# Other step costs in a planner, a later ranking of the experts, and a last block in two halves

## The chip, the cores and the metric

The kernel runs on one core of a Trainium2 chip. Its time is the device time of one execution in microseconds (us), a median over runs. The core's engines run beside each other and wait for one another through semaphores: TensorE (PE in the profile; its weight loads are PEld), VectorE (DVE), ScalarE (ACT), GpSimd (POOL) and SyncE (SP), which issues most transfers. Each engine works through its own list of instructions strictly in order.

## The reference

Three parts follow each other. (1) Causal attention for 4 batches x 8 heads, 576 positions, head size 64, with a bias from a running sum. (2) A gated projection: five taps of a causal convolution give a gate, and the output is `(gate * (x @ w_val)) @ w_out`. (3) A layer of eight experts: each of 2304 tokens goes to one expert.

```python
bias = -(cum[:, :, :, None] - cum[:, :, None, :])
scores = np.where(causal, -1e9, scale * q @ k.T + np.minimum(bias, 0.0))
x = softmax(scores) @ v                            # attention, 32 heads
for k in range(5): gate_pre += conv_w[k] * xp[:, k:k + S, :]
x = sigmoid(gate_pre) * (x @ w_val) @ w_out        # gated projection
e = fresh_e if s == 0 or local_gate[b, s] < 0.5 else prev_e
out[b, s] = p[e] * (np.maximum(x[b, s] @ w1[e], 0.0) @ w2[e])
```

## The kernel before

Products that need full precision are made of three products of split operands (a high part and a rest, names with `h` and `l`).

**First part.** It covers attention, projection, logits and routing. The 32 heads are taken as 16 pairs, numbered 0 to 15, four to a batch. For each pair: q and k are loaded, transposed on TensorE, split by ACT and DVE into the single tile `qk` (lines 531 and 535), and copied into `T_p`; from pair 7 on all six copies of a pair are transfers of SP (`COPY`, L600). Nine score tiles `s_p_u` (L659 to L683) are read by DVE, which writes `tt` and the row minima (L666, L690), go through the exponential on ACT (L699), are scaled on POOL (L724), transposed on TensorE (`t`, L736), copied by ACT to `PT0` and `PT1` (L746 to L754) and multiplied by v (`pv_p`, L789). ACT copies the result to `x_p` (L799), of which there are two buffers. `x_p` is split by POOL (`xh`, `xl`, L803 and L807) and goes through the five taps on DVE (`g_p`, L814 once and L816 four times) and the gate's function on ACT (L821). A buffer of `x` is free again when the taps and the split of its pair have read it.

For each batch b, eight groups `val_b` of 12 matmuls (L866) are made, each followed by `y` and `yl` on DVE (L872, L890) and `yh` on ACT. Then come the groups `x2_b` of 12 matmuls (L927): the second half of the columns with the logits (`lgs`, L939), and the first half. These groups belong to no pair, so they can stand between the steps of later pairs. `route(b)` finds the expert and the slot of each token (L986 to L1055).

**What sets the order.** Every piece is a `Step` with an engine, a cost, what it comes after, the buffers that it holds (`SIZES`), and a rank (`RANKS`, a table of offsets that puts a step relative to its pair; the taps have pair + 31.589, pv has pair - 2.111). `Plan.order` counts time forward: it keeps a free time for each engine, takes the ready step that can start first, the one of lowest rank among those an engine could start at once, and adds its cost. It doubles the cost of a TensorE step when the window before was filled too little. The order found is then written out; on the chip only the order is left of the costs.

**Routing of the last batch.** `rank` and `back` give the slots. `excess` sorts the experts by their load (`turns`), sixteen short DVE steps L1170 to L1187 after a small product `nb` (L1160). `match` (L1065) and `own` (L1073) find expert 0's tokens, `join` (L1077, L1079) writes their list `id0`. Then POOL gathers the first tokens' rows (`xg`, L1306).

**Second part.** `ffn` takes the experts in turn: `up` (L1344), `down` (L1419, or L1385 turned), `leave` (L1361 on DVE, L1363 on ACT, then a scatter of the rows by POOL, L1365). At the end `over` loads the count of left-over blocks into every engine's register (L1192) and branches on it (L1193).

Of the kernel before, what the change touches and what calls it, by code (L numbers as in the profile page):

```python
# [22 lines left out]
P = 128  # L23
# [13 lines left out]
def fv(ap):  # L37
    return ap.bitcast(F32)
# [131 lines left out]
def build(tc, q, k, v, s, w_val, conv_w, w_out, w_gate, w_local, w1, w2, out, dbg=None):  # L170
    nc = tc.nc
    with ExitStack() as ctx:
# [35 lines left out]

# [300 lines left out]
        def qk_main(p, nm, loaded, sn):  # L509
# [26 lines left out]
            t = add("PE", 1.05 if p in LAY else 0.43, turn, loaded, ready["ident"], qk_read.get((p - 1, ih)), on=[sn, sm])  # L536
            a = add("ACT", 0.5, hi, t, qk_read.get((p - 1, ih)), on=[sm])
            z = add("DVE", 0.62, lo, a, qk_read.get((p - 1, il)), on=[sm])
            return a, z
# [34 lines left out]
        def assemble(p, k_, q_, r_):  # L574
# [15 lines left out]
            for h in range(2):  # L590
                r = slice(64 * h, 64 * h + 64)
                hd[h] = []
                for n, (a, i, src) in enumerate(((0, 0, slice(1, 3)), (64, 0, slice(0, None, 2)), (0, 1, slice(1, None, 2)))):
# [3 lines left out]
                    def copy(a=a, i=i, src=src, r=r, h=h, how=how):  # L597
# [7 lines left out]
                        else:  # L605
                            nc.gpsimd.tensor_scalar(o, fv(z), 1.0, 1.0, ALU.mult, ALU.mult)
                    hd[h].append(add(*{"S": ("SP", 0.91), "A": ("ACT", 1.12), "D": ("DVE", 0.74), "P": ("Pool", 1.25)}[how],
                                     copy, begun, deps, on=[sT], lat=FAR if how == "S" else 0.17))
# [9 lines left out]
        def attention(p):  # L618
# [20 lines left out]
            def unit(u):  # L639
# [31 lines left out]
                else:  # L671
                    m = None
                    for z in range(2):
# [12 lines left out]
                        def least(z=z, c=c):  # L686
                            if z == 0:
# [151 lines left out]
            g_done[p] = add("ACT", 0.57, gate, m, on=[sg]), sg  # L839

# [6 lines left out]
        def value(b, ranks, after=None, sm_tag="m"):  # L847
# [5 lines left out]
            for i in range(8):  # L853
# [39 lines left out]
                m = add("PE", c_pe(12 * 288), prod, al, [x[0] for x in xd], [w_done[j] for j in range(4)],  # L893
                        on=[sm] + [sl for x in xd for sl in x[1]])
# [5 lines left out]
                h = add("ACT", c_act(288) + 0.14 * more, hi, e, w_conv if more else None, on=on)  # L900
                l_ = add("DVE", c_dve(288) + 0.065 * more, lo, h, on=on)
                y_steps.setdefault((b, z), []).extend([h, l_])

        def x2_tile(b, t, ranks):
# [11 lines left out]
            for c0, c1, rank in ((256, WO, ranks[0]), (0, 256, ranks[1])):  # L916
# [24 lines left out]
                def store(c0=c0, tl=tl):  # L941
                    if both:
# [5 lines left out]
                    nc.sync.dma_start(out=x2d[r:r + m, c0:c0 + 256], in_=tl["x2"][0:m])  # L948
                a = add("PE", c_pe(12 * (c1 - c0)), prod, y_steps[b, 0], y_steps[b, 1] if t > 1 else None,
                        y_steps[0, 1] if both else None, [w_done[j] for j in range(4, 8)],  # L950
# [134 lines left out]
        def route(b):  # L1085
# [71 lines left out]
        def excess(part):  # L1157
# [121 lines left out]
        def ffn():  # L1279
# [13 lines left out]
            def blocks(e):  # L1293
                return [(n, min(P, BUD[e] - P * n)) for n in range((BUD[e] + P - 1) // P)]
# [78 lines left out]
            def down_wide(e, h):  # L1373
# [30 lines left out]
                late.extend(lambda n=n, m=m: back(n, m) for n, m in blocks(e))  # L1404

            def down(e, h):

                if turned(e):
                    return down_wide(e, h)
                for n, m in blocks(e):  # L1410
                    ps = bank()
                    c = slice(P * n, P * n + m)
# [14 lines left out]
                    leave(e, n, m, ps, DM // 2 if e == E - 1 and last else DM if n % 2 else 0)  # L1427

# [113 lines left out]
```

## Time and profile before

| | |
|---|---|
| median of 3 runs | 638.65 us (638.48 to 641.74) |
| the profiled execution | 637.11 us |
| its span, first to last instruction | 635.3 us |
| granted TensorE clock, mean | 0.956 |
| busy share of the span: PE, DVE, ACT, POOL | 92%, 65%, 55%, 39% |
| first part, up to the first product of `ffn` | 385.5 us |

A row of a view by stretches gives the busy time of each engine in that stretch, with its number of instructions in brackets, the granted clock (1.00 is full, 0.50 half) and the share that the transfer engines were busy. A busy TensorE is not one at its peak.

### The profile page before, as it was taken

The page shows a single profiled execution, that of the slowest core. Times are in us where ns is not written, and L with a number is a line of the kernel's source. Part 1 is how long each engine was busy: PE and PEld are TensorE (multiplying, and loading weights), DVE is VectorE, ACT ScalarE, POOL GpSimd, SP SyncE. Part 2 cuts the span into 40 slices and gives each one's busy share as a digit, 9 for nine tenths or more (in the row PEclk, how much of TensorE's full clock was granted, in tenths as well). Part 3 has the DMA queues.
Part 4 walks back from the last instruction along what each step waited for, and adds up shares of the span by engine and source line. Part 5 has one row for each costly group of instructions (what it writes and reads, how often), then busy time and mean ns, then how long its engine had stood idle before and what let it go on. Part 6 is the DMA issues. An engine that isn't in the chain of part 4 may idle for free.

```text
span 635.3 us, 12047 instructions
## 1 busy us (share of the span) xinstructions
PE 587.1 (92%) x4104; PEld 518.7 (82%) x4104; DVE 413.1 (65%) x1024; ACT 347.8 (55%) x867; POOL 248.3 (39%) x376
## 2 busy tenths in 40 slices
PE   6697988999999999988989978999999999999993
PEld 5475766778778887867979978899898999999792
DVE  5589897888866898974779434435363636465440
ACT  4487786877667777755635304424343536355440
POOL 7367786642634365546541242030403003132101
PEclk8899798999999999989989969999999999999997
DMA  8877467766588787736044624355464637375610
GB/s 160 160 181 181 107 141 151 147 157 135 139 198 200 164 187 168 165 94 150 18 156 131 105 46 135 111 182 164 161 195 145 205 100 247 117 235 173 233 46 26
DMA packets 94244, 93.94 MB, mean 148 GB/s; under 512 B 62040, under 2 KB 68312, under 8 KB 94120
## 3 DMA queue, kind: packets, MB, share of 16 engines
q1 hardware_dynamic: 90244, 83.15, 51.3%
q0 software_dynamic: 3936, 9.99, 5.0%
q8 instruction: 34, 0.56, 0.4%
q14 instruction: 30, 0.25, 0.2%
HBM read 57.90 MB, written 10.79 MB: 108 GB/s over the span
## 4 chain that ended last, share of the span: by engine, by line
PE 60%; DVE 19%; issue 8%; DMA 7%; POOL 3%; ACT 2%; SPq 1%; POOLq 0%; DVEq 0%; ACTq 0%
PE h L1344 15%; PE h L1419 8%; PE h L1385 7%; PE x L927 5%; PE val L866 5%; PE pv L789 4%; DMA T<-qk 4%; DVE g L816 3%; PE t L736 3%; DVE tt L666 3%; PE s L659 2%; PE s L661 2%; PE xT L1321 1%; POOL tt L724 1%; DVE qk L535 1%
## 5 line engine op out<-in xcount | busy, mean ns | idle before, releaser
L724 POOL TENSOR_SCALAR tt<-tt,st 128x512 f32<-128x512 f32 (+1 forms) x144 | 99.8, 708 | 98.1 <-ACT tt L699 45.9
L1276 DVE TENSOR_TENSOR wl<-raw,wh 128x1024 fp32r<-128x1024 f32 x64 | 78.2, 1223 | 32.3 <-ACT wh L1273 31.5
L699 ACT ACTIVATE tt<-tt,st 128x512 f32<-128x512 f32 (+3 forms) x144 | 83.4, 581 | 21.8 <-DVE st L666 12.1
L1344 PE MATMUL h<-xth,wh 128*128 128x384 f32 (+5 forms) x256 | 76.0, 311 | 1.4 <-ACT xth L1323 1.4
L1344 PE MATMUL h<-xth,wl 128*128 128x384 f32 (+5 forms) x256 | 75.1, 308 | 0.0
L1365 POOL DMA_INDIRECT out_dram<-out,id x22 | 28.0, 1273 | 114.0 <-ACT out L1363 93.7
L736 PE MATMUL t<-ident,tt 128*128 128x128 f32 x384 | 64.8, 285 | 6.3 <-POOL tt L724 2.9
L666 DVE CUSTOM_DVE_ANT_0 tt<-s,mask 128x512 f32<-128x512 f32 (+3 forms) x128 | 59.0, 484 | 14.9 <-PE s L661 12.9
L1273 ACT ACTIVATE wh<-raw 128x1024 fp32r<-128x1024 f32 x64 | 66.7, 1053 | 0.0
L1349 DVE SCALAR_TENSOR_TENSOR hl<-h,hh 128x384 fp32r<-128x384 f32 (+5 forms) x64 | 31.2, 487 | 45.5 <-ACT hh L1348 45.3
L1348 ACT ACTIVATE hh<-h 128x384 fp32r<-128x384 f32 (+5 forms) x64 | 28.1, 438 | 57.9 <-PE h L1344 54.1
L816 DVE SCALAR_TENSOR_TENSOR g<-x,cw,g 128x576 f32<-128x576 f32 x64 | 58.3, 914 | 0.5
L736 PEld LDWEIGHTS t<-ident,tt 128*128 128x128 f32 x384 | 47.2, 146 | 13.6 <-POOL tt L724 6.2
L1306 POOL DMA_INDIRECT xg<-x2d,id x22 | 22.6, 1029 | 83.4 <-PE h L1402 42.6
L659 PE MATMUL s<-T 128*128 128x256 f32 (+2 forms) x128 | 48.8, 388 | 6.9 <-DVE st L690 5.0
L789 PE MATMUL pv<-PT,nv 128*64 128x320 f32 (+3 forms) x384 | 50.0, 392 | 2.3 <-ACT x L799 2.0
L1344 PEld LDWEIGHTS h<-xth,wh 128*128 128x128 f32 x256 | 48.1, 188 | 1.9 <-ACT xth L1323 1.6
L1344 PEld LDWEIGHTS h<-xth,wl 128*128 128x128 f32 x256 | 48.1, 188 | 0.2
L1344 PE MATMUL h<-xtl,wh 128*128 128x384 f32 (+5 forms) x256 | 47.7, 308 | 0.0
L661 PE MATMUL s<-T 68*128 68x256 f32 (+2 forms) x128 | 42.9, 344 | 3.0 <-DMA T<-qk 2.9
L789 PEld LDWEIGHTS pv<-PT,nv 128*64 128x64 f32 x384 | 26.2, 138 | 22.3 <-issue 4.1
L927 PE MATMUL x<-wo_h,yl 128*128 128x266 f32 (+3 forms) x144 | 43.1, 299 | 0.0
(236 smaller groups left out, 1577.5 us busy)
## 6 DMA issues: line engine op xcount, KB each, us to landing
raw<-in_moe_w_dram SPq DMA_DIRECT2D x64, 512.0 KB
T<-qk SPq DMA_DIRECT2D x76, 320.0 KB
nv<-in_v_dram SPq DMA_DIRECT2D x32, 128.0 KB
x2d<-x SPq DMA_DIRECT2D x32, 128.0 KB
nk<-in_k_dram SPq DMA_DIRECT2D x26, 128.0 KB
nq<-in_q_dram SPq DMA_DIRECT2D x26, 128.0 KB
wsc<-in_moe_w_val_dram SPq DMA_DIRECT2D x4, 512.0 KB
wsc<-in_moe_w_out_dram SPq DMA_DIRECT2D x4, 512.0 KB
```

Source lines behind the costliest of these rows:

```text
L659: nc.tensor.matmul(ps[:, 0:N], lhsT=Q[:, 0, P * t:P * t + P], rhs=K[:, 0, 0:N], start=True, stop=False)
L661: nc.tensor.matmul(ps[:, 0:N], lhsT=Q[0:68, 1, P * t:P * t + P], rhs=K[0:68, 1, 0:N], start=False, stop=True)
L666: nc.vector.tensor_tensor_reduce(out=tl["tt"][:, 0:W], in0=tl["ps"][:, 0:W], in1=mask[:, 512 - W:512], scale=1.0, scalar=3.0e38, op0=ALU.a ...
L699: nc.scalar.activation(tt[:, 0:W], tt[:, 0:W], AF.Exp, bias=st[:, 0, i:i + 1], scale=-1.0, accum_out=st[:, 1, i:i + 1])
L724: nc.gpsimd.tensor_scalar(tl["tt"][:, 0:W], tl["tt"][:, 0:W], st_["st"][:, 2, i:i + 1], 1.0, ALU.mult, ALU.mult)
L736: nc.tensor.transpose(ps[:, j], tl["tt"][:, P * j:P * j + P], ident)
L789: nc.tensor.matmul(tl["ps"][64 * h:64 * h + 64, half, c:c + w], lhsT=vt[0:K, j, h] if j < 4 else vr[:, 2 * hp + h], rhs=(PT1 if half else ...
L816: nc.vector.scalar_tensor_tensor(tl["g"], x[:, t:t + S], cw[:, hp, t:t + 1], tl["g"], ALU.mult, ALU.add)
L927: nc.tensor.matmul(ps[0:m, 0:c1 - c0], lhsT=yy[:, kc] if both else yy[:, kc, P * t:P * t + m], rhs=wt_[:, kc, c0:c1], start=n == 0, stop=n ...
L1273: nc.scalar.activation(hi, raw, AF.Copy)
L1276: nc.vector.tensor_tensor(lo, raw, fv(hi), ALU.subtract)
L1344: nc.tensor.matmul(ps[:, 0:N], lhsT=w[:, P * f:P * f + P], rhs=xx[:, kc, 0:N], start=n == 0, stop=n == 11)
```

## The change

Three edits.

1. The planner's costs. `c_pe`, `c_act`, `c_dve` and `c_pool` give a step other fixed parts and slopes, and single steps get other numbers: a tap of DVE 0.88 for 0.73 (the first one 0.8 for 0.4), POOL's split 0.72 and 1.5 for 0.65 and 1.36, the copies into `T` more on every engine. `RANKS`, `SIZES` and what comes after what are the same, so the instructions of the first part are the same and their order on each engine differs.
2. `nb` and `excess` come after `join`.
3. The last block of the last expert is made in two halves of 256 columns, each with its own copy (DVE for the first, ACT for the second) and its own scatter, and the count for `over` is loaded before the second copy.

```diff
-        def c_pe(n):
-            return n / 2350
+        def c_pe(n, k=2):
+            return n / 2400 + 0.0125 * k
         def c_act(n):
-            return 0.05 + n / 1200
+            return 0.12 + n / 1200
         def c_dve(n):
-            return 0.065 + n / 960
+            return 0.11 + n / 960
         def c_pool(n):
-            return 0.23 + n / 1000
+            return 0.35 + n / 950
...
-            a = add("Pool", 0.65, hi, xo, on=[sx, sh])
-            z = add("Pool", 1.36, lo, a, on=[sx, sh, sl])
+            a = add("Pool", 0.72, hi, xo, on=[sx, sh])
+            z = add("Pool", 1.5, lo, a, on=[sx, sh, sl])
...
-                m = add("DVE", 0.73 if t else 0.4, lambda t=t: tap(t), xo, m, ready["cw"], on=[sx, sg])
+                m = add("DVE", 0.88 if t else 0.8, lambda t=t: tap(t), xo, m, ready["cw"], on=[sx, sg])
...
-            add("DVE", 0.4, lambda: one[b].join(), m, base, on=[sm])
+            joined = add("DVE", 0.4, lambda: one[b].join(), m, base, on=[sm])
...
-            a = add("PE", 0.1, lambda: excess(0), ranked, on=[sm])
+            a = add("PE", 0.1, lambda: excess(0), ranked, joined, on=[sm])
...
+            def down_end(e, h, n, m):
...
+                for z in range(2):
+                    nc.vector.tensor_scalar(it2[0:m, z:z + 1], it[0:m, n, 0:1], 2, z, ALU.mult, ALU.add)
+                for z in range(2):
+                    ps = bank()
...
+                            nc.tensor.matmul(ps[0:m, 0:256], lhsT=a[:, c], rhs=w[:, r], start=k == 0, stop=k == 23)
...
+                    if z:
+                        fa["most"] = blocks_left()
...
+                    if z:
+                        nc.scalar.activation(o[0:m, 0:256], ps[0:m, 0:256], AF.Copy, scale=p)
+                    else:
+                        nc.vector.tensor_scalar(o[0:m, 0:256], ps[0:m, 0:256], p, None, ALU.mult)
+                    nc.gpsimd.memset(spare, 0.0)
+                    i = nc.gpsimd.indirect_dma_start(
+                        out=out.rearrange("b s (z d) -> (b s z) d", z=2),
...
```

Where the order moves, first DVE in the middle of the first part, around the last tap of pair 9 (`g_9`; `tt_p_u` is a score read of pair p, `y` and `yl` belong to a `val` group, `lgs` to an `x2` group). Before:

```order
L816 SCALAR_TENSOR_TENSOR g_9_3053<-x_9_2892,cw_97,g_9_3053 128x576
L690 ISA tt_11_2_3119,st_11_0_3079<-s_11_2_1_3157,mask4_82,st_11_0_3079 128x288
L690 ISA st_11_0_3079 128x1
L535 SCALAR_TENSOR_TENSOR qk_103<-qT_12_3149,qk_103 128x512
L666 ISA tt_11_3_3183,st_11_1_3182<-s_11_3_3174,mask_81 128x512
```

And in the changed kernel:

```order
L666 ISA tt_14_5_3710,st_14_1_3659<-s_14_5_3684,mask_81 128x256
L666 ISA st_14_1_3659 128x1
L872 SCALAR_TENSOR_TENSOR y_1_3_1_3712<-g_7_2544,val_1_3_1_3662 128x288
L816 SCALAR_TENSOR_TENSOR g_9_3542<-x_9_2802,cw_97,g_9_3542 128x576
L711 TENSOR_SCALAR st_14_1_3659<-st_14_1_3659 128x3
...
L939 COPY lgs_1_157<-x2_1_0_256_3727 128x9
L814 TENSOR_SCALAR g_10_3769<-x_10_3022,cw_97 128x576
L816 SCALAR_TENSOR_TENSOR g_9_3542<-x_9_2802,cw_97,g_9_3542 128x576
L939 COPY lgs_0_155<-x2_1_4_256_3752 64x9
L939 COPY lgs_1_157<-x2_1_4_256_3752 64x9
L816 SCALAR_TENSOR_TENSOR g_9_3542<-x_9_2802,cw_97,g_9_3542 128x576
```

The last tap of pair 9 stood among the score reads of pair 11; now it stands behind six of the nine score reads of pair 14.

Second, ACT at the end of attention, around the copy of pair 15's first product (`x_15`). Before:

```order
L746 ACTIVATE PT0_104<-t_15_7_4506 128x256
L933 ACTIVATE x2_2_1_256_4545<-x2_2_1_256_4513 128x256
L821 ACTIVATE g_14_4497<-g_14_4497 128x576
L799 ACTIVATE x_15_4566<-pv_15_4533 128x320
L746 ACTIVATE PT0_104<-t_15_8_4551 128x128
```

And in the changed kernel:

```order
L821 ACTIVATE g_13_4415<-g_13_4415 128x576
L799 ACTIVATE x_15_4531<-pv_15_4503 128x320
L746 ACTIVATE PT0_104<-t_15_7_4525 128x256
L746 ACTIVATE PT0_104<-t_15_8_4529 128x128
L933 ACTIVATE x2_2_1_256_4555<-x2_2_1_256_4534 128x256
L799 ACTIVATE x_15_4531<-pv_15_4503 128x256
L821 ACTIVATE g_14_4522<-g_14_4522 128x576
```

The gate of pair 14 (`g_14`) stood ahead of both copies of `x_15` and now stands behind them.

Third, DVE after the last batch's slots are known (`mx_3`): `sh_3` is the first of the sixteen steps of `excess`, `eq` are the five of `match`. Before, and then in the changed kernel:

```order
L1044 TENSOR_REDUCE mx_3_5020<-so_3_5129 128x5
L1170 SCALAR_TENSOR_TENSOR sh_3_5021<-nb_5137,pref_85 1x8
L1171 MEMSET sh_3_5021 1x1
...
L1187 CAST nbo_108<-sh_3_5021 1x8
L1065 TENSOR_SCALAR eq_0_5171<-slot_no_4614,mx_3_5020 128x384
```

```order
L1044 TENSOR_REDUCE mx_3_5020<-so_3_5129 128x5
L1065 TENSOR_SCALAR eq_0_5151<-slot_no_4593,mx_3_5020 128x384
...
L1079 TENSOR_TENSOR id0_89<-id0_89,own_5185 128x3 x2
L1171 SCALAR_TENSOR_TENSOR sh_3_5021<-nb_5205,pref_85 1x8
...
L1188 CAST nbo_108<-sh_3_5021 1x8
L1328 TENSOR_TENSOR xtl_0_5321<-xT_0_0_5322,xth_0_5320 128x4x128
```

The sixteen steps of `excess` moved from in front of `match` to behind `join`. The first gather of `ffn` waits, in both kernels, for the last DVE instruction that stands ahead of `ffn`: that was L1079, and is now L1188.

Counted over whole stretches of the order, cut behind the last scores of a pair: between pairs 0 and 7, 7 and 8, 8 and 13, 13 and 15, and behind pair 15 up to the last routing product `so_3`, TensorE's list held 6, 5, 20, 9 and 28 groups of `val` and `x2` (8 + 12 `val` + `x2` in the third, 6 + 3 in the fourth); it now holds 5, 3, 14, 14 and 32 (6 + 8 and 4 + 10). The products `pv_12` moved from the third to the fourth. DVE's list, cut behind the last score reads of the same pairs, held 24, 7, 20, 1 and 12 of the taps of L816; it now holds 19, 4, 13, 16 and 12. The fourth stretch also gets 5 more `yl`, 6 more `lgs` and a second routing.

## Rows read from the trace of the kernel before

**Rows 1.** Busy time by stretches; cut at last score reads of pairs 0, 7, 8, 13, 15

```profile
core 0: us, PE busy (x) PEld busy (x) DVE busy (x) ACT busy (x) POOL busy (x), PEclk, DMA share, GB/s
34.50:155.40 120.90, 109.33 (x782) 87.76 (x780) 105.20 (x304) 93.25 (x278) 75.69 (x101) 0.93 0.64 146
155.40:177.90 22.50, 21.71 (x166) 18.82 (x164) 20.50 (x55) 15.26 (x47) 14.48 (x18) 1.00 0.70 163
177.90:269.20 91.30, 89.18 (x682) 75.04 (x683) 72.56 (x237) 66.51 (x207) 43.93 (x67) 1.00 0.77 179
269.20:311.85 42.65, 38.84 (x284) 32.87 (x283) 27.22 (x97) 24.91 (x78) 20.16 (x36) 0.96 0.43 102
311.85:366.30 54.45, 52.45 (x413) 49.65 (x411) 41.10 (x92) 23.08 (x59) 18.05 (x25) 0.97 0.43 117
385.50:625.40 239.90, 238.27 (x1480) 222.19 (x1480) 119.91 (x159) 105.73 (x163) 48.35 (x62) 1.00 0.50 161
```

**Rows 2.** Chain of waits: start us, length us, engine, tile, line, instructions

```profile
182.65 2.35 PE pv L789 x20
186.64 0.80 PE pv L789 x8
189.04 1.42 PE x L927 x12
197.98 1.60 PE val L866 x12
477.30 11.13 PE h L1419 x48
578.47 1.38 PE h L1344 x12
```

**Rows 3.** The taps' line: instructions, duration ns min/median/max

```profile
L816 DVE SCALAR_TENSOR_TENSOR g<-x,cw,g x64: 781/819/1883, 49.5 to 332.6; 128x576 f32<-128x576 f32 x64
```

**Rows 4.** Timeline of POOL and of DVE: start us, length us, instructions

```profile
318.43 3.21 POOL L807 TENSOR_TENSOR xl<-x,xh 128x576 fp32r<-128x576 f32 x2
...
320.38 2.74 DVE L816 SCALAR_TENSOR_TENSOR g<-x,cw,g 128x576 f32<-128x576 f32 x2
```

**Rows 5.** Busy time by stretches of 2 us, behind pair 15

```profile
324.00:326.00 2.00, 0.08 (x1) 0.08 (x2) 0.89 (x2) 1.14 (x4) 0.00 (x0) 1.00 0.18 66
326.00:328.00 2.00, 2.00 (x14) 1.77 (x15) 0.52 (x1) 0.69 (x3) 0.54 (x1) 0.79 0.35 86
328.00:330.00 2.00, 2.00 (x11) 2.00 (x11) 1.26 (x2) 0.26 (x1) 1.94 (x4) 0.50 0.92 320
```

**Rows 6.** Timeline of ACT behind pair 15; in brackets idle time and releaser

```profile
324.86 0.68 ACT L821 ACTIVATE g<-g 128x576 f32<-128x576 f32 x1 [1.25 <-DVE g L816]
325.45 0.42 ACT L799 ACTIVATE x<-pv 128x320 f32<-128x320 f32 x1
```

**Rows 7.** Timeline of the last routing

```profile
366.47 0.15 DVE L1170 SCALAR_TENSOR_TENSOR sh<-nb,pref 1x8 f32<-1x8 f32 x1
...
369.22 0.28 PE L927 MATMUL x<-wo_h,yh 128*64 128x256 f32 x1
...
369.61 1.72 DVE L1065 TENSOR_SCALAR eq<-slot_no,mx 128x384 fp32r<-128x384 f32 x5
...
372.29 3.33 PE L1073 MATMUL own<-tv,eq 128*128 128x4 f32 x15 [2.79 <-DVE tv L1134]
...
376.62 1.01 POOL L1306 DMA_INDIRECT xg<-x2d,id  x1 [1.18 <-issue]
```

**Rows 8.** Timeline of the end

```profile
624.92 0.40 PE L1419 MATMUL h<-wh,hh 128*128 128x512 f32 x1
625.36 0.48 DVE L1361 TENSOR_SCALAR out<-h,id 128x256 f32<-128x256 f32 x1 [10.35 <-PE h L1419]
625.92 0.47 ACT L1363 ACTIVATE out<-h,id 128x256 f32<-128x256 f32 x1 [5.48 <-DVE out L1361]
626.67 0.98 POOL L1365 DMA_INDIRECT out_dram<-out,id  x1 [4.90 <-ACTq L1193]
```

More of the change, by code (lines that the diff above doesn't have):

```diff
@@ L536, in qk_main @@
             t = add("PE", 1.05 if p in LAY else 0.43, turn, loaded, ready["ident"], qk_read.get((p - 1, ih)), on=[sn, sm])
-            a = add("ACT", 0.5, hi, t, qk_read.get((p - 1, ih)), on=[sm])
-            z = add("DVE", 0.62, lo, a, qk_read.get((p - 1, il)), on=[sm])
+            a = add("ACT", 0.56, hi, t, qk_read.get((p - 1, ih)), on=[sm])
+            z = add("DVE", 0.66, lo, a, qk_read.get((p - 1, il)), on=[sm])
             return a, z
@@ L606, in copy @@
                             nc.gpsimd.tensor_scalar(o, fv(z), 1.0, 1.0, ALU.mult, ALU.mult)
-                    hd[h].append(add(*{"S": ("SP", 0.91), "A": ("ACT", 1.12), "D": ("DVE", 0.74), "P": ("Pool", 1.25)}[how],
+                    hd[h].append(add(*{"S": ("SP", 0.91), "A": ("ACT", 1.2), "D": ("DVE", 1.05), "P": ("Pool", 1.6)}[how],
                                      copy, begun, deps, on=[sT], lat=FAR if how == "S" else 0.17))
@@ L693, in least @@
                                 accum_out=st[:, 0 if z else 3, i:i + 1])
-                        o = add("PE", c_pe(4 * 288), prod, Td[0], Td[1], on=[sT, sp], rows=0.77)
+                        o = add("PE", c_pe(4 * 288, 4), prod, Td[0], Td[1], on=[sT, sp], rows=0.77)
                         m = add("DVE", c_dve(288), least, o, m, ready["mask"], on=[sp, stt, ss])
@@ L712, in rec @@
                     nc.vector.reciprocal(st[:, 2, 0:n], st[:, 1, 0:n])
-                r = add("DVE", 0.3, rec, exps, on=[ss])
+                r = add("DVE", 0.4, rec, exps, on=[ss])
                 for i in range(n):
@@ L837, in attention @@
             for t in range(5):
-                m = add("DVE", 0.73 if t else 0.4, lambda t=t: tap(t), xo, m, ready["cw"], on=[sx, sg])
-            g_done[p] = add("ACT", 0.57, gate, m, on=[sg]), sg
+                m = add("DVE", 0.88 if t else 0.8, lambda t=t: tap(t), xo, m, ready["cw"], on=[sx, sg])
+            g_done[p] = add("ACT", 0.64, gate, m, on=[sg]), sg
         yb, y_steps, y_free, lgs, lg_steps = {}, {}, {}, {}, {}
@@ L892, in value @@
                 gd, sg = g_done[b * NP + oc]
-                m = add("PE", c_pe(12 * 288), prod, al, [x[0] for x in xd], [w_done[j] for j in range(4)],
+                m = add("PE", c_pe(12 * 288, 12), prod, al, [x[0] for x in xd], [w_done[j] for j in range(4)],
                         on=[sm] + [sl for x in xd for sl in x[1]])
@@ L900, in value @@
                 h = add("ACT", c_act(288) + 0.14 * more, hi, e, w_conv if more else None, on=on)
-                l_ = add("DVE", c_dve(288) + 0.065 * more, lo, h, on=on)
+                l_ = add("DVE", c_dve(288) + 0.1 + 0.065 * more, lo, h, on=on)
                 y_steps.setdefault((b, z), []).extend([h, l_])
@@ L948, in store @@
                     nc.sync.dma_start(out=x2d[r:r + m, c0:c0 + 256], in_=tl["x2"][0:m])
[L949 removed]
+                a = add("PE", c_pe(12 * (c1 - c0), 12), prod, y_steps[b, 0], y_steps[b, 1] if t > 1 else None,
                         y_steps[0, 1] if both else None, [w_done[j] for j in range(4, 8)],
@@ L1189, in excess, with blocks_left @@
                 nc.sync.dma_start(out=nbd.rearrange("(o e) w -> o e w", o=1), in_=nbo)
+        def blocks_left():
+            return nc.values_load(most_, min_val=0, max_val=(NT - BUD[-1]) // P)
         def over():
-            most = nc.values_load(most_, min_val=0, max_val=(NT - BUD[-1]) // P)
+            most = fa["most"]
             with tc.If(most > 0):
@@ L1404, in down_wide @@
                 late.extend(lambda n=n, m=m: back(n, m) for n, m in blocks(e))
+            def down_end(e, h, n, m):
+                it = idt[e]
+                p = fv(it)[0:m, n, 1:2]
+                c = slice(P * n, P * n + m)
+                it2 = fx.tile([P, 2], I32, tag="it2", name="halves", bufs=1)
+                for z in range(2):
+                    nc.vector.tensor_scalar(it2[0:m, z:z + 1], it[0:m, n, 0:1], 2, z, ALU.mult, ALU.add)
+                for z in range(2):
+                    ps = bank()
+                    k = 0
+                    for f in range(8):
+                        wh, wl = wt[e, 4 + f // 2]
+                        r = slice(DM * (f % 2) + 256 * z, DM * (f % 2) + 256 * z + 256)
+                        hh, hl = h[f]
+                        for a, w in ((hl, wh), (hh, wl), (hh, wh)):
+                            nc.tensor.matmul(ps[0:m, 0:256], lhsT=a[:, c], rhs=w[:, r], start=k == 0, stop=k == 23)
+                            k += 1
+                    if z:
+                        fa["most"] = blocks_left()
+                    o = fx.tile([P, DM], F32, tag="o", name=f"out_{e}_{n}_{z}", bufs=3)
+                    if z:
[5 more added lines that the diff above has]
+                        out=out.rearrange("b s (z d) -> (b s z) d", z=2),
+                        out_offset=bass.IndirectOffsetOnAxis(ap=it2[0:m, z:z + 1], axis=0), in_=o[0:m, 0:256],
+                        in_offset=None, bounds_check=2 * NT - 1, oob_is_err=False)
+                    tc.declare_no_dep(i.ins, group="rows", reason="rows differ")
+                    tc.add_to_no_dep_group("rows", i.ins)
             def down(e, h):
@@ L1410, in down @@
                 for n, m in blocks(e):
+                    if e == E - 1 and n == len(blocks(e)) - 1:
+                        down_end(e, h, n, m)
+                        return
                     ps = bank()
@@ L1426, in down @@
                             w_next()
-                    leave(e, n, m, ps, DM // 2 if e == E - 1 and last else DM if n % 2 else 0)
+                    leave(e, n, m, ps, DM if n % 2 else 0)
             order = [(e, i) for e in range(E) for i in range(8)][4:]
```

## The prediction

> **What bounds the kernel now.** I read the busy time by stretches first, cut where DVE has read the last score of a pair, then the chain of waits, then the timelines of three places. The stretches [rows 1] are: S1 (pairs 0 to 7, 120.90 us), S2 (to pair 8, 22.50), S3 (to pair 13, 91.30), S4 (to pair 15, 42.65), S5 (from there to the last routing product, 54.45), then the last routing up to 385.5 us, then the experts (239.90). In S1 DVE has the least slack that matters: 105.20 of 120.90 us, 87%. In S2 and S3 TensorE does: 21.71 of 22.50 and 89.18 of 91.30, with DVE at 72.56 and the transfers at 0.77. S4 is TensorE again, 38.84 of 42.65, with DVE at only 27.22. S5 is TensorE, 52.45 of 54.45. The experts keep TensorE at 238.27 of 239.90 us at full clock. So the planner's order decides S1 to S5, 331.8 us in which the binding engine changes, and the two small edits decide some us at the joint and at the end.
>
> The total work does not change. Every gain of the first edit is idle time of the binding engine that goes away, or work that moves from a stretch where its engine binds to one where it does not.
>
> **First edit, stretch by stretch.** The prices: a `val` group takes 1.60 us of TensorE, an `x2` group 1.42, a pair's two pv products 2.35 + 0.80 = 3.15 [rows 2]; a tap 0.82 us of DVE (median) [rows 3].
>
> S1: DVE loses five L816 taps (24 to 19), one L814, one `y` and three `yl`, in all 5 x 0.82 = 4.1 plus about 2. With 87% of the stretch busy I count most of it: -5 us; bounds -6 (DVE paces all of it) and 0 (the chain of a pair paces it).
>
> S2: three `x2` groups leave and one `val` comes, -3 x 1.42 + 1.60 = -2.7 us of an engine busy 96% of the time. I take -2.5; bounds -3 and 0.
>
> S3: two `val` and four `x2` groups leave, and pair 12's products with them: -3.2 - 5.7 - 3.15 = -12.0 us of TensorE, 77.1 left. What is late next is ACT, 66.51 now and about 62 then, and the transfers, 0.77 x 91.30 = 70 us that do not shrink. At the share that TensorE has now the stretch would end 12.3 us earlier; the transfers would then be busy 89% of the time, more than in any stretch of rows 1, so I take -11. Bounds -12.3 and 0 (the copies into `T` pace the pairs).
>
> S4 pays. It gets two `val` groups less, seven `x2` more and pair 12's products, -3.2 + 9.9 + 3.15 = +9.9 us for TensorE (48.7). DVE gets fifteen taps, two first taps, five `yl`, six `lgs` and one routing: 15 x 0.82 = 12.3, and about 11 for the rest by the same line prices, so 27.2 + 23 = 50 us. DVE becomes the engine that ends last. At the 0.91 that TensorE reaches there now, 50 us make 55: +12.4. The near bound is 50.2 us, DVE without a gap (+7.6). The far one is the lowest share that DVE has in a neighbouring stretch where it also works through taps, `y` and routing, S5 with 41.10 / 54.45 = 0.755: 66 us (+23). I take 55 because S4, like S1, would have the score reads in between, and S1 runs at 0.87.
>
> Here a tap's price is weighed once more. Two taps under POOL's two splits took 2.74 us, 1.37 each, against the 0.82 of the median [rows 3, 4]. The Trainium skill (SBUF — State Buffer, section "SBUF: two separate sides") says why that would be: a DVE instruction with two inputs in SBUF and a GpSimd instruction take the same port pair in turns, and the loser blocks. The trace agrees with it here. By it the planner's fixed 0.88 for a tap is too low wherever POOL works; POOL would be busy some 32 us of S4's 55 (its 20.16 and about 12 for a second set of sends and three more splits), so 0.58 x 15 x 0.55 = 4.8 us more for S4 and 639.2 us in all. The sum below stays with 0.91, since S1's 24 taps under a POOL busy 75.69 of 120.90 us are part of its 87%.
>
> S5: four `val` groups more, +6.4 us. Against them, the stall behind pair 15: TensorE stands 1.92 us in 324 to 326, and the granted clock is 0.79 and 0.50 in the 4 us behind it, 2 x (0.21 + 0.50) = 1.4 us lost [rows 5]. It stands because ACT's copy of `x_15` at 325.45 is queued behind the gate of pair 14 at 324.86, which waited 1.25 us for the taps [rows 6]; in the new order that gate stands behind the copies. The four groups fill what is left of the stall, so 6.4 - 3.3 = +3.1; bounds 0 and +6.4.
>
> Sum of the first edit: -5 - 2.5 - 11 + 12.4 + 3.1 = -3.0 us.
>
> **Second edit.** `excess` takes 369.61 - 366.47 = 3.14 us of DVE ahead of `match` [rows 7]. Without it `match` starts 3.1 us earlier, its 1.72 us and the five short steps behind it end near 369.2, and `own` starts at 369.5, where TensorE's last `x2` matmul ends, instead of 372.29. That is 2.8 us earlier. But the gather now waits for the last instruction of `excess`, so the 3.14 us stand behind `join` again: own's end, 3.14, and the 1.0 us that lie between own's end and the gather now. With own's 3.33 us that gives 377.0, 0.4 later than 376.62. `own` ran there at half clock, after TensorE had stood for 2.79 us; where it follows the `x2` matmuls at once it may take half of its time, 1.7 us, and the gather starts at 375.3, 1.3 earlier. I take -0.8; bounds -1.3 and +0.4. `turns`, written some 5 us later, is first read for expert 1's weights, which are loaded behind the first products of `ffn`: hidden.
>
> **Third edit.** 48 matmuls of 256 columns for 24 of 512: 48 x 1.38 / 12 = 5.5 us against 24 x 11.13 / 48 = 5.6 [rows 2], so nothing. DVE's half and its scatter lie beside the second half's matmuls. After the last matmul ACT no longer waits for DVE's copy: now 625.36 to 625.92 passes before it starts [rows 8], then not. Gain 0.56; the count's loads are short and beside other work. The rest, from POOL's scatter to the end of the span, moves with it. I take -0.5; bounds -0.8 and 0. The two steps for the halved row numbers lie on DVE, which has stood 10.35 us there.
>
> **The total.** -3.0 - 0.8 - 0.5 = -4.3. Made against the profiled execution's own 637.11 us that is 632.8. The median of the runs shown is 638.65, 1.54 above it, and so the forecast is 638.65 - 4.3 = 634.4 us.
>
> **Rivals.**
>
> *Nothing moves.* The time that the binding engines need, DVE in S1 and S4 and TensorE elsewhere, is about the same in both orders (the sum of the moved amounts, with S4 at DVE's 50 us, is -6 - 2.7 - 12 + 50 - 38.8 + 6.4 = -3), and the gaps of S4 eat it. For it: S1 to S5 already run at 87 to 98% of the binding engine. Against it: the stall in S5 has a cause that the new order takes away. Time: 637.5.
>
> *Slower: the taps hold the pairs.* Place: S4, the last tap of pair 9. There are two `x` buffers, so pair 11's copy waits for it, pair 12's products for that copy, and so on to pair 15. DVE's list now has six score reads of pair 14, four `y` and their `yl` ahead of that tap, and behind it two routings, each a chain from TensorE over ACT to DVE during which DVE stands. If DVE gets under a share of about 0.80 of S4 (62 us) the first edit loses; at S5's 0.755 S4 takes 66 us, 11 more than I count. Time: 634.4 + 11 = 645.4. For it: a rank that puts the taps last, now with more of DVE's time known as taken. Against it: TensorE's groups lie there as filler, and S1 kept 0.87 with the same taps.
>
> *Much faster.* S1 to S3 reach their near bounds and S4 takes 52 us: -6 - 3 - 12.3 + 9.4 + 0 = -12, and -1.8 for the two other edits: 624.8. For it: dense attention leaves no engine over 90% in S3. Against it: transfers near 0.9.
>
> That the new costs leave the order nearly as it was is ruled out by the order itself.
>
> **How the numbers follow.** The forecast case, 630.5 to 637, has 0.42; nothing moves 0.19; slower 0.25; much faster 0.14. A measurement of this kernel tells about 0.5%, 3.2 us, from no change: below 635.5 is faster, above 641.8 slower. Faster: 0.14, four fifths of 0.42 and a little of the second, 0.50. Slower: 0.26 with the rival's own. Same: 0.24. The range, 623 to 646, reaches from the much faster case to the slower one; the far ends of all bounds together lie outside it.
>
> **What would show it.** In the changed profile: S3 (score reads of pair 8 to those of pair 13) near 80 us with the transfers above 0.80; S4 near 55 us with DVE above 0.85 busy; no standing of TensorE behind pair 15 and no half clock there; the first gather less than 9.6 us after the last routing product; ACT's last copy starting within 0.1 us of the last matmul. I am wrong if S3 does not shrink by more than 5 us, or if S4 takes more than 62.

## The result, and the profile after

The changed kernel takes 644.56 us (median of 16 runs, 640.05 to 649.26) against 640.25 us for the kernel before (16 runs). The ratio on record is 1.0085, 95% interval 1.0063 to 1.0107, which is 5.4 us slower; the two medians lie 4.3 us apart. The forecast was 4.3 us faster. The profiled execution took 642.79 us with a span of 641.0 us, 5.7 us above that of before, so the profiles show about the median difference.

The stretches first, cut at the same events as in [rows 1]: last score reads of pairs 0, 7, 8, 13 and 15, then the last routing product; the last row is the experts. Busy time by stretches, after:

```profile
core 0: us, PE busy (x) PEld busy (x) DVE busy (x) ACT busy (x) POOL busy (x), PEclk, DMA share, GB/s
35.20:155.95 120.75, 107.74 (x767) 84.36 (x766) 99.60 (x298) 89.92 (x272) 75.78 (x99) 0.93 0.68 155
155.95:176.65 20.70, 18.52 (x130) 15.05 (x128) 16.02 (x48) 13.05 (x42) 8.62 (x13) 0.92 0.86 167
176.65:255.50 78.85, 75.81 (x572) 63.93 (x572) 58.04 (x194) 60.56 (x193) 34.30 (x56) 1.00 0.87 188
255.50:314.05 58.55, 52.82 (x403) 44.66 (x401) 49.39 (x143) 32.45 (x102) 31.21 (x42) 0.97 0.37 87
314.05:373.30 59.25, 57.59 (x454) 53.90 (x452) 44.46 (x103) 23.65 (x62) 22.94 (x35) 1.00 0.41 107
392.00:631.00 239.00, 238.53 (x1497) 223.90 (x1496) 120.11 (x160) 105.73 (x163) 50.49 (x64) 0.99 0.51 162
```

S1 is as long as it was (120.75 against 120.90), although DVE has 5.6 us less to do in it. S2 is 1.8 us shorter, S3 12.45 shorter, S4 15.9 longer, S5 4.8 longer, and S1 begins 0.7 later: +7.0 at the last routing product. The two small edits give some of it back.

One profile is not enough for terms of 1 to 5 us, and the experiments gave more of each order (of each only the stretches that its edit leaves alone, cut at the same events):

| stretch | old order, us (profiles) | new order, us (profiles) | difference of means | forecast |
|---|---|---|---|---|
| S1 | 120.7 to 121.5 (4) | 119.6 to 121.7 (6) | -0.2 | -5 |
| S2 | 22.5 to 22.7 (6) | 18.2 to 22.6 (6) | -1.5 | -2.5 |
| S3 | 91.3 to 95.1 (4) | 78.6 to 79.1 (5) | -14.2 | -11 |
| S4 | 40.0 to 43.5 (5) | 58.6 to 58.8 (3) | +16.9 | +12.4 |
| S5 | 54.0 to 54.6 (5) | 58.6 to 59.4 (6) | +4.8 | +3.1 |

The differences sum to +5.8 us where -3.0 was forecast. S2 of the new order goes with the granted clock: 18.2 us in e1, where it was 1.00, and 22.4 in e12, where it was 0.85.

The last routing, timeline after (start, length, engine, line):

```profile
373.61 1.74 DVE L1065 TENSOR_SCALAR eq<-slot_no,mx 128x384 fp32r<-128x384 f32 x5
...
376.31 1.81 PE L1073 MATMUL own<-tv,eq 128*128 128x4 f32 x15
...
378.63 0.15 DVE L1171 SCALAR_TENSOR_TENSOR sh<-nb,pref 1x8 f32<-1x8 f32 x1
...
381.68 0.15 DVE L1188 CAST nbo<-sh 1x8 int32<-1x8 f32 x1
382.72 1.00 POOL L1310 DMA_INDIRECT xg<-x2d,id  x1 [3.27 <-issue]
```

`own` follows the x2 matmuls at once and takes 1.81 us, not 3.33 [rows 7], at a granted clock of 1.00 instead of 0.50; `excess` then stands ahead of the gather as forecast. From the last routing product to the gather it is 382.72 - 373.30 = 9.4 us, before 376.62 - 366.30 = 10.3.

The end, timeline after:

```profile
631.77 0.27 PE L1427 MATMUL h<-wh,hh 128*128 128x256 f32 x1
632.08 0.47 ACT L1433 ACTIVATE out<-h,id 128x256 f32<-128x256 f32 x1 [4.98 <-PE h L1427]
632.83 0.98 POOL L1437 DMA_INDIRECT out_dram<-out,halves  x1 [1.77 <-ACTq L1197]
```

ACT starts 0.04 us behind the last matmul, before 0.60 behind it [rows 8]. From the end of POOL's instruction to the end of the span it is 641.0 - 633.81 = 7.2 us, before 635.3 - 627.65 = 7.65: with half the columns the span ends sooner behind the scatter too (7.2 in e2 as well). So the third edit gives 1.0 us.

Behind pair 15 the half clock is gone, and the stand of TensorE is shorter and lies elsewhere. Busy time by stretches of 2 us, after, to be held against [rows 5]:

```profile
320.00:322.00 2.00, 0.93 (x7) 0.73 (x6) 1.20 (x3) 0.45 (x1) 2.00 (x5) 1.00 0.01 0
324.00:326.00 2.00, 2.00 (x19) 2.00 (x18) 2.00 (x4) 1.19 (x4) 1.63 (x2) 1.00 0.00 0
326.00:328.00 2.00, 2.00 (x18) 1.60 (x18) 2.00 (x3) 1.19 (x5) 2.00 (x2) 1.00 0.04 8
```

### The profile page after: what moved, and what is told of

Same layout as the page of the kernel before. It is cut to its first block, busy times and chain, and to the rows that moved or that the text cites. A ratio compares the mean times of both kernels' runs of the same rounds, so it can differ in the third digit from the quotient of the medians.

```text
span 641.0 us, 12128 instructions
## 1 busy us (share of the span) xinstructions
PE 588.6 (92%) x4128; PEld 518.3 (81%) x4128; DVE 414.3 (65%) x1026; ACT 344.5 (54%) x867; POOL 250.8 (39%) x378
## 4 chain that ended last, share of the span: by engine, by line
PE 68%; DMA 11%; DVE 9%; ACT 4%; SPq 3%; issue 3%; POOL 1%; POOLq 0%; ACTq 0%; DVEq 0%
PE h L1348 17%; PE h L1460 10%; PE x L927 8%; PE h L1389 6%; PE val L866 6%; DMA T<-qk 5%; PE pv L789 5%; PE t L736 4%; DMA wsc<-in_moe_w_out_dram 2%; PE s L659 2%; PE xT L1325 2%; SPq L600 2%; DVE tt L666 1%; PE s L661 1%; ACT tt L699 1%
## 5 line engine op out<-in xcount | busy, mean ns | idle before, releaser
L724 POOL TENSOR_SCALAR tt<-tt,st 128x512 f32<-128x512 f32 (+1 forms) x144 | 95.7, 678 | 110.2 <-DVE st L712 52.6
L699 ACT ACTIVATE tt<-tt,st 128x512 f32<-128x512 f32 (+1 forms) x144 | 83.4, 583 | 19.9 <-DVE st L666 16.8
L816 DVE SCALAR_TENSOR_TENSOR g<-x,cw,g 128x576 f32<-128x576 f32 x64 | 63.9, 1002 | 0.2
L659 PE MATMUL s<-T 128*128 128x256 f32 (+2 forms) x128 | 50.3, 399 | 9.9 <-DVE st L690 6.2
L1310 POOL DMA_INDIRECT xg<-x2d,id x22 | 23.9, 1085 | 84.6 <-DMA id<-ids 34.9
L1348 PEld LDWEIGHTS h<-xth,wl 128*128 128x128 f32 x256 | 48.7, 190 | 0.2
L789 PEld LDWEIGHTS pv<-PT,nv 128*64 128x64 f32 x384 | 25.8, 140 | 22.4 <-issue 5.1
L927 PE MATMUL x<-wo_h,yl 128*128 128x256 f32 (+3 forms) x144 | 42.5, 295 | 0.5 <-ACT x L933 0.5
```

The source lines that it names most:

```text
L659: nc.tensor.matmul(ps[:, 0:N], lhsT=Q[:, 0, P * t:P * t + P], rhs=K[:, 0, 0:N], start=True, stop=False)
L699: nc.scalar.activation(tt[:, 0:W], tt[:, 0:W], AF.Exp, bias=st[:, 0, i:i + 1], scale=-1.0, accum_out=st[:, 1, i:i + 1])
L724: nc.gpsimd.tensor_scalar(tl["tt"][:, 0:W], tl["tt"][:, 0:W], st_["st"][:, 2, i:i + 1], 1.0, ALU.mult, ALU.mult)
L789: nc.tensor.matmul(tl["ps"][64 * h:64 * h + 64, half, c:c + w], lhsT=vt[0:K, j, h] if j < 4 else vr[:, 2 * hp + h], rhs=(PT1 if half else ...
L816: nc.vector.scalar_tensor_tensor(tl["g"], x[:, t:t + S], cw[:, hp, t:t + 1], tl["g"], ALU.mult, ALU.add)
L927: nc.tensor.matmul(ps[0:m, 0:c1 - c0], lhsT=yy[:, kc] if both else yy[:, kc, P * t:P * t + m], rhs=wt_[:, kc, c0:c1], start=n == 0, stop=n ...
```

## The experiments

**Which edit loses: runs e1 and e2.** The first puts the first edit alone on the kernel before, the second takes it out of the changed kernel.

```diff
-        def c_pe(n):
-            return n / 2350
+        def c_pe(n, k=2):
+            return n / 2400 + 0.0125 * k
...
-                m = add("DVE", 0.73 if t else 0.4, ...
+                m = add("DVE", 0.88 if t else 0.8, ...
```

Expected of e1: 

> The kernel before with the first edit alone (the planner's costs); excess and the last block as before. Theory A (the whole loss is the first edit's; the two others gain 1.9 us as their rows say): some 6 to 8 us over before, ratio 1.010 to 1.013, last routing product 6 to 8 us later than in before. Theory B (the late excess delays the experts' part, the first edit costs little): ratio 1.000 to 1.004.

Expected of e2: 

> The changed kernel with the first edit undone, so the late excess and the halved last block on the old order. Theory A: 1.3 to 1.9 us under before, ratio 0.997 to 0.998, first gather 9.3 to 9.6 us behind the last routing product, last matmul to end of span 9.0 us. Theory B: 2 to 4 us over before, ratio 1.003 to 1.006.

Measured: e1 1.0152 (1.0122 to 1.0182), e2 0.9979 (0.9948 to 1.0009). Theory A holds: the first edit loses it all, in e1 a little more than the 1.010 to 1.013 expected. One sign of theory A failed: in e1's profile the last routing product comes 1.7 us later than in before (368.0 against 366.3), not 6 to 8. That execution, of 638.31 us, is e1's shortest, 7.8 under its median, so it can't stand for the others. The two other edits together are worth about -1.3 us by e2's ratio, which the interval alone doesn't tell from nothing; e2's profile repeats their rows (9.4 us from the last routing product to the gather, 9.0 from the last matmul to the end). e2 has the lowest ratio of the study: no slower than before, and 1% under the changed kernel.

**What paces S1: runs e4, e5, e6 and e15.** All stand on the kernel before in its own order. e4 leaves out the last tap of pairs 0 to 4, e5 two thirds of the products of `val` in the first batch, e15 both; e6 adds matmuls in S1.

```diff
-                m = add("DVE", 0.73 if t else 0.4, lambda t=t: tap(t), ...
+                m = add("DVE", 0.73 if t else 0.4, lambda t=t: tap(t) if t < 4 or p > 4 else None, ...
...
-                        for wt_, xx in ((wv_h, xl), (wv_l, xh), (wv_h, xh)):
+                        for wt_, xx in ((wv_h, xl), (wv_l, xh), (wv_h, xh))[:3 if b else 1]:
```

```diff
+                    if b == 0 and 4 * z + oc < 5:
+                        for kc in range(4):
+                            xh, xl = xhl[b * NP + kc]
+                            for i, xx in enumerate((xl, xh)):
+                                nc.tensor.matmul(ps[:, 0:288], lhsT=wv_h[:, kc, oc * P:(oc + 1) * P], rhs=xx[:, c], ...
```

Expected of e4: 

> The kernel before, in its own order, with the last tap of pairs 0 to 4 left out: five taps, 4.1 us of DVE, all of them in S1 (between the last score reads of pair 0 and pair 7). If DVE paces S1, as the prediction counted it, S1 is 3 to 5 us shorter than 120.9 and the time 3 to 5 us less, ratio 0.992 to 0.995. If TensorE or the chain of a pair paces it: S1 within 1 us of 120.9, ratio 0.999 to 1.001.

Expected of e5: 

> The kernel before, in its own order, with 8 of the 12 matmuls left out in each of the eight val groups of the first batch: 64 matmuls, 64 x 0.133 = 8.5 us of TensorE, seven groups (7.5 us) in S1 and one in S2. If TensorE paces S1: S1 5 to 7.5 us shorter than 120.9, ratio 0.988 to 0.992. If DVE or the chain of a pair paces it: S1 0 to 2 us shorter, ratio 0.996 to 1.000.

Expected of e6: 

> The kernel before with 40 matmuls more, none of whose results is used: the first five val groups of the first batch, all in S1, run eight matmuls of 288 columns more each, 40 x 0.133 = 5.3 us of TensorE at full clock. Theory C (S1 and S2 have room on TensorE, so work that leaves them gains nothing there and costs its full price where it goes): the time changes by 0 to 1.5 us, ratio 1.000 to 1.002. Rival (TensorE paces S1 too): 4 to 5.3 us more, ratio 1.006 to 1.008.

Expected of e15: 

> The kernel before with both removals of two runs above at once: the five taps and the 64 matmuls. Read by S1 alone, since the left out products change the routing and so the experts' part. Theory F (S1 is paced by the chain of each pair, through ACT, POOL and the transfers): S1 within 1 us of 120.9. Rival (TensorE and DVE each have work that covers the other's absence, and pace it together): S1 3 to 7 us shorter.

Busy time of S1 by the same cuts, columns as above; first in e4, with five taps less:

```profile
34.30:156.00 121.70, 109.09 (x786) 87.67 (x784) 100.46 (x301) 92.89 (x278) 74.53 (x100) 0.93 0.63 144
```

In e5, with products less:

```profile
35.10:156.10 121.00, 106.52 (x733) 83.27 (x729) 105.78 (x304) 92.85 (x277) 75.48 (x100) 0.92 0.64 146
```

In e15, with both less:

```profile
34.57:158.23 123.66, 106.88 (x733) 83.12 (x730) 99.12 (x300) 92.89 (x277) 74.59 (x100) 0.90 0.63 143
```

In e6, with 40 matmuls more:

```profile
35.26:159.01 123.75, 112.20 (x827) 91.59 (x825) 104.87 (x305) 93.55 (x278) 76.61 (x101) 0.94 0.64 144
```

No removal shortens S1: 121.70, 121.00 and 123.66 us against 120.90. TensorE's busy time falls by less than the work left out: by 2.8 us in e5, where 49 matmuls less at 0.133 are 6.5, with a granted clock of 0.92 (0.90 in e15) against 0.93. More work does lengthen S1, by 2.9 us for 5.3. The time of e4 says the same (1.0025, 0.9996 to 1.0053). That of e6 (1.0021, 0.9992 to 1.0050) ends below the 1.006 of its rival, so it speaks for theory C, though S1 itself grew by half of the price. The times of e5 and e15 say nothing, since the routing changes. So neither DVE nor TensorE nor the two together pace S1, by the amounts that were left out. Theory F, that the chain of each pair does (through ACT, POOL and the transfers), is what is left and not shown: nothing was left out on those engines, and e15's S1, a single execution, missed its band of 1 us by 1.8.

**The price of TensorE's work in S3: run e7.** The edit of e6 with `b == 1`.

Expected: 

> The same 40 matmuls, but in the first five val groups of the second batch, which lie in S3 of the kernel before. Theory C (TensorE paces from S3 on): 4 to 5.3 us more, ratio 1.006 to 1.008. Rival (TensorE has room there too): under 1.5 us, ratio below 1.002.

Busy time of S3 in e7:

```profile
178.08:276.42 98.34, 94.39 (x716) 80.00 (x717) 72.10 (x237) 66.22 (x207) 42.72 (x66) 1.00 0.71 162
```

98.3 us against 91.3 to 95.1 in four profiles without the extra work, mean 93.0: 5.3 us more than the mean, for 5.3 us of matmuls, and 3.2 more than the longest. The time moved less, 1.0034 (1.0002 to 1.0066), which is below what was expected; the stretch agrees with theory C, the time can't tell.

**What paces S4: runs e12, e13 and e14.** All three stand on the changed kernel. e12 leaves out the last two taps of pairs 9 to 11, e13 two thirds of the products in five `x2` groups, and e14 moves two splits of POOL.

```diff
-                m = add("DVE", 0.88 if t else 0.8, lambda t=t: tap(t), ...
+                m = add("DVE", 0.88 if t else 0.8, lambda t=t: tap(t) if t < 3 or p not in (9, 10, 11) else None, ...
...
+                        few = b == 1 and c0 == 0
+                        for yy, wt_ in ((yl, wo_h), (yh, wo_l), (yh, wo_h))[2 * few:]:
```

```diff
             order = plan.order()
+            late = [plan.steps[i] for i in (1270, 1366)]
+            order = [s for s in order if s[1] not in late]
+            at = 1 + next(n for n, s in enumerate(order) if s[1] is plan.steps[1804])
+            order[at:at] = [(0.0, st) for st in late]
```

Expected of e12: 

> The changed kernel with the last two taps of pairs 9, 10 and 11 left out: six taps, 4.9 us of DVE at the median of before, all in S4. Theory D (the taps hold the pairs in S4): S4 4 to 6 us under 58.6 and the time about that much less, ratio to before 0.999 to 1.003. Theory C (TensorE paces S4): S4 within 1.5 us of 58.6, ratio to before 1.006 to 1.010.

Expected of e13: 

> The changed kernel with 8 of 12 matmuls left out in the five x2 groups of the second batch's first half of columns, which lie in S4 of the changed kernel: 40 matmuls, 40 x 0.118 = 4.7 us of TensorE. Theory C: S4 and S5 together 3.5 to 4.7 us under 117.8, ratio to before 1.001 to 1.004. Theory D (the pairs wait for taps and TensorE has room): 0 to 1.5 us, ratio 1.006 to 1.010.

Expected of e14: 

> The changed kernel with two POOL steps, the splits xl of pairs 9 and 10, moved behind three scalings of pair 14. In the changed kernel they ran from 267.93 to 271.21 us, a tap beside them took 1.94 us and a step of 128x3 elements 1.36, and TensorE then stood for 2.31 us. Theory E (a POOL split holds DVE, DVE holds the logits' copy, that holds TensorE): the 128x3 step takes 0.2 us, TensorE's gap there falls from 2.31 us to under 0.8, S4 is 1.5 to 2.3 us under 58.6, ratio to before 1.004 to 1.008. Rival (S4 has a length of its own, whatever one engine does): the gap goes or moves and S4 stays within 0.7 us of 58.6, ratio 1.006 to 1.011.

Busy time of the whole of S4 in e12:

```profile
257.10:315.70 58.60, 52.84 (x403) 44.66 (x402) 45.39 (x139) 32.31 (x102) 29.21 (x42) 0.97 0.37 86
```

Its two halves, cut at the last score read of pair 14, in the changed kernel:

```profile
255.50:294.00 38.50, 32.95 (x244) 27.60 (x242) 32.60 (x86) 18.24 (x59) 19.55 (x22) 0.96 0.47 110
294.00:314.05 20.05, 19.86 (x162) 17.06 (x161) 16.79 (x59) 14.21 (x43) 11.66 (x21) 1.00 0.18 42
```

The same halves in e13:

```profile
254.90:293.70 38.80, 32.36 (x236) 26.29 (x233) 33.23 (x87) 19.25 (x61) 16.76 (x24) 0.96 0.48 110
293.70:311.85 18.15, 17.09 (x130) 13.78 (x129) 16.83 (x59) 13.18 (x42) 11.45 (x18) 1.00 0.19 45
```

Six taps less leave S4 at 58.6 us (e12's time: 1.0120, 1.0079 to 1.0161), so the taps' time alone does not set it. In e13 the second half, where TensorE is busy 99%, shrinks by 1.9 us, and the first half, where it is busy 86%, not at all (38.50 and 38.80), though three of the five groups stand there. S4 and S5 together end 1.8 us under 117.8, between the two theories' bands, and the time lies between them too, 1.0057 (1.0029 to 1.0085). The first half is where S4 grew: the kernel before took 288.85 - 269.20 = 19.65 us for it.

The end of that first half shows what takes the place of the work left out. Where DVE waits for TensorE's routing product (`mx<-so`), with the last score read of pair 14 behind it, in the changed kernel (timeline):

```profile
290.57 2.26 DVE L816 SCALAR_TENSOR_TENSOR g<-x,cw,g 128x576 f32<-128x576 f32 x3
293.15 0.20 DVE L1044 TENSOR_REDUCE mx<-so 128x5 f32<-128x40 f32 x1 [0.32 <-PE so L1041]
```

In e12, where that group has two taps less:

```profile
291.27 1.10 DVE L816 SCALAR_TENSOR_TENSOR g<-x,cw,g 128x576 f32<-128x576 f32 x1
294.84 0.20 DVE L1044 TENSOR_REDUCE mx<-so 128x5 f32<-128x40 f32 x1 [2.47 <-PE so L1041]
```

And in e13, with its products less (its lines are numbered one higher):

```profile
291.09 2.26 DVE L816 SCALAR_TENSOR_TENSOR g<-x,cw,g 128x576 f32<-128x576 f32 x3
293.28 0.19 DVE L1045 TENSOR_REDUCE mx<-so 128x5 f32<-128x40 f32 x1
```

With the taps away DVE stands 2.47 us for TensorE; with the products away it does not wait at all, and the taps fill the time up to there. So at that place the two engines are within 0.32 us of each other, and each covers the other's absence. Whether S4 shrinks when both are left out at once, as e15 tried for S1, was not run.

Theory D has a second half that e12 does not test: that a late tap holds the `x` buffer. The third tap of pair 9 stays where it was. In the changed kernel the last tap of pair 9 and the copies of pair 11 (the fifth pair from the last in ACT's list) are these:

```profile
275.48 0.81 DVE L816 SCALAR_TENSOR_TENSOR g<-x,cw,g 128x576 f32<-128x576 f32 x1
...
277.35 0.23 ACT L995 ACTIVATE pr<-sh 128x40 f32<-128x40 f32 x1
277.47 0.70 ACT L799 ACTIVATE x<-pv 128x256 f32<-128x256 f32 x2
```

The copies start 1.2 us after the tap has ended, directly behind the instruction ahead of them in ACT's list, and in e12 they start as far into S4 as here (22.1 and 22.0 us). So on the chip they wait for their place in ACT's list and not for the taps. Whether another place in the lists for pair 9's taps and pair 11's copies would shorten S4 was not tried.

The longest stand of TensorE in that half, in the changed kernel (timeline):

```profile
267.93 3.29 POOL L807 TENSOR_TENSOR xl<-x,xh 128x576 fp32r<-128x576 f32 x2
268.02 1.94 DVE L816 SCALAR_TENSOR_TENSOR g<-x,cw,g 128x576 f32<-128x576 f32 x1
269.88 1.36 DVE L711 TENSOR_SCALAR st<-st 128x3 f32<-128x3 f32 x1
272.08 0.15 DVE L939 COPY lgs<-x 128x9 f32<-128x9 f32 x1
272.29 0.39 PE L927 MATMUL x<-wo_h,y_rest 128*128 128x266 f32 x1 [2.31 <-DVE lgs L939]
```

And the same instructions in e14:

```profile
268.58 2.67 POOL L724 TENSOR_SCALAR tt<-tt,st 128x384 f32<-128x384 f32 x3
268.89 0.88 DVE L816 SCALAR_TENSOR_TENSOR g<-x,cw,g 128x576 f32<-128x576 f32 x1
269.69 0.15 DVE L711 TENSOR_SCALAR st<-st 128x3 f32<-128x3 f32 x1
270.69 0.16 DVE L939 COPY lgs<-x 128x9 f32<-128x9 f32 x1
```

The mechanism of theory E is there: with the splits away, the tap takes 0.88 and the small step 0.15 us, and TensorE's 2.31 us of standing are gone (a stand of 1.22 comes a little later). But S4 only goes from 58.55 to 57.8 us, a third of it and just beyond the rival's 0.7, and the time (1.0118, 1.0071 to 1.0165) does not show it.

**Other orders: runs e8, e9, e10 and e11.** e8 raises only the taps' costs; e9 is the changed kernel with ranks chosen anew by the planner's own counted end; e10 and e11 join one plan up to the last score product of pair 9 to the rest of the other.

```diff
-RANKS = dict(pv=-2.111, split=3.54, tap=31.589, ...
+RANKS = dict(pv=-15.805, split=3.375, tap=54.931, ...
...
-            order = plan.order()
+            order = [(0.0, plan.steps[i]) for i in JOINED]
```

Expected of e8: 

> The kernel before with only the planner's cost of the taps raised, 0.4 to 0.8 and 0.73 to 0.88. In this order TensorE's list has 8 groups of val and x2 up to pair 7 and 13 up to pair 8, where before has 6 and 11 and the changed kernel 5 and 8. Theory C (what counts is how much of TensorE's work lies ahead of the last scores of pair 8): two groups more ahead, 0 to 3 us faster than before, ratio 0.995 to 1.001. Rival (the ranks fit the old costs alone, so that any other cost makes an order that is worse by some us): 5 to 8 us slower, ratio 1.008 to 1.013.

Expected of e9: 

> The changed kernel, all three edits, with the planner's table of ranks chosen anew for the new costs. TensorE's list has 5 groups of val and x2 up to pair 7, 10 up to pair 8 and 27 up to pair 13 (before 6, 11, 31; changed 5, 8, 22). Theory C: one group fewer than before ahead of pair 8, 1.5 us lost, less the 1.3 to 1.9 us of the two small edits: ratio 0.997 to 1.003. Rival (the new costs themselves are what misleads, with any ranks): 4 to 8 us slower than before, ratio 1.006 to 1.012.

Expected of e10: 

> The kernel before, all else unchanged, with its first part in a joined order: the steps of the old plan up to the last score product of pair 9, then the others as the new plan has them. Theory C (the first edit loses in S1 and S2, where less of TensorE's work fits in nearly the same time): 0 to 2 us over before, ratio 1.000 to 1.003. Theory D (it loses behind, in S4, where pair 12 waits for the taps of pair 9): 5 to 9 us over before, ratio 1.008 to 1.014.

Expected of e11: 

> The other joint: the new plan's steps up to the last score product of pair 9, then the others as the old plan has them. Theory C: 4 to 9 us over before, ratio 1.006 to 1.014. Theory D: 0 to 2 us, ratio 1.000 to 1.003.

Measured: e8 1.0059 (1.0021 to 1.0097), between the two theories; e9 1.0065 (1.0029 to 1.0100), at the near end of the rival's; e10 1.0253 (1.0206 to 1.0300) and e11 1.0157 (1.0103 to 1.0210). Theories C and D each wanted one joined order near 1.000, and neither is. The joint has a price of its own: in e11 pair 9 alone takes 202.2 - 177.9 = 24.3 us, in the two whole plans 17.1 and 17.6. So the joined orders decide nothing between C and D. What stays is that every order that the planner made with other costs was slower than the old one, e9's with new ranks too.

## Why the prediction was wrong

The step that failed is the price of S1: "With 87% of the stretch busy I count most of it: -5 us". DVE's busy time fell as counted, from 105.20 to 99.60 us, and the stretch did not move. [rows 1] could have warned: TensorE at 109.33 and DVE at 105.20 of 120.90 are two engines that are both busy and both not full, and nothing there says that either paces. e4, e5 and e15 show that neither does. The bound of 0 that stood beside it was the right end; that "the chain of a pair paces it", as it says, is argued and not shown. By the means S1 is 4.8 us of the 8.8 that lie between the forecast of -3.0 and +5.8; S4 is 4.5, S5 1.7 and S2 1.0, and S3 went 3.2 the other way.

The second step is S4, sized by DVE at a share of 0.91. DVE's 50 us were right (49.39), but it reached a share of 0.84. TensorE's 48.7 us were 4.1 short of the measured 52.82: the rows of S4 hold 119 matmuls more than before, where the groups and products counted make 88, and 15 of the others are the second routing's (L1016 and L1041), which the count gave to DVE alone. S4 lasted 58.55 us, 3.5 over the 55 of the forecast and inside its bounds. Its first half takes 38.5 us, and at its end TensorE and DVE take turns as the one that is waited for (e12, e13); what would shorten it is open. Behind S4, S5 got its four groups at +4.8 us of their 6.4.

The table's column of differences says where the gain went. TensorE's matmuls are the same in both kernels. S1 and S2 hold 51 fewer of them (948 before, 897 after in the rows) and are only 1.7 us shorter by the means; S3, S4 and S5 together, which run them later, are 7.5 us longer (-14.2 + 16.9 + 4.8). By the stretches the idle time of TensorE from S1 to the last routing product went from 331.80 - 311.51 = 20.3 to 338.1 - 312.5 = 25.6 us (22.6 in e2's profile of the old order, 25.7 in e1's of the new). The forecast had taken the idle time to fall.

The other steps, in the prediction's order:

- S2: -1.5 by the means for -2.5; between 18.2 and 22.6 us in six profiles, it moves by more than that.
- S3: near 80 us with the transfers above 0.80 was to be seen; it is 78.85 and 0.87. "TensorE" as the pace of S3 is right in the old order (e7); it was not tried in the new one.
- S5: no half clock there, as said; the stand is 1.07 us (2.00 - 0.93) instead of 1.92, so less of the 6.4 us was won back than the 3.3 counted.
- The last routing: -0.9 for -0.8, `own` at 1.81 us where 1.7 was guessed.
- The end: -1.0 for -0.5. The 0.56 us of ACT came; that the span also ends 0.46 us sooner behind a scatter of half the columns was not counted.
- The port: the prediction added 0.55 us per tap under POOL for 4.8 us more and left it out of its sum. By the list of costliest groups all 64 taps took 63.9 us against 58.3 before. One place of it was tried in S4: a tap and a tiny step beside POOL's splits cost TensorE 2.31 us, of which 0.8 came back in e14. The Trainium skill (SBUF — State Buffer, section "SBUF: two separate sides") says that the holder keeps the shared ports for a whole instruction and that a DVE operation in a two-port mode asks for them as well; the step of 128x3 with one input, 1.36 us beside the split and 0.15 without it, fits that if it runs in such a mode, which no run here shows.

The prediction's own two signs of being wrong did not show, since S3 shrank by 12.45 us and S4 stayed under 62. Of its signs of being right two failed, DVE above 0.85 busy in S4 (0.84) and no standing of TensorE behind pair 15 (1.07 us).

The slower rival named 645.4 us, close to 644.56, but not for its reason: S4 did not reach its 66 us, pair 11's copies did not wait for pair 9's taps, and six taps less did not shorten it. The time was near by luck, a sum of other errors.

## What to carry to other kernels

A stretch gets shorter by the work that leaves it only if that work paces it, and a busy share of 87 or 90% does not say so: leave the work out on the chip, once per engine and once on both, before a price is put on it. Costs nearer to the traced durations need not give a faster order: a tap took 0.91 us on the mean in the kernel before, its cost went from 0.73 to 0.88, and the new costs alone made the kernel 1.5% slower. Choosing the ranks again with them did not bring it back; why is open. When work moves between stretches, add up the idle time of the engine with the most work over all of them, not the gain of each.

## What was not expected of the hardware

A DVE instruction of 128x3 elements took 1.36 us beside a two-input POOL instruction and 0.15 us away from it, and a tap 1.94 instead of 0.88. Leaving matmuls out of S1 took 2.8 us off TensorE's busy time there where 6.5 us of work had gone (e5), and made the stretch no shorter; the granted clock was 0.92 in e5 and 0.90 in e15 against 0.93, and since S1 of the new order shows 0.92 to 0.96 with nothing left out, only e15's lies outside, in one execution. The halved last scatter let the span end 7.2 us behind POOL's instruction instead of 7.65 (7.17 to 7.23 in five profiles, 7.61 to 7.70 in five of the whole scatter).
